# Regrouping the small matmuls of a chunked state-space scan among the matmuls of an MLP

## The chip, the cores and the metric

One NeuronCore of a Trainium2 chip runs the kernel. The metric is the device time of one execution in microseconds (us), as a median of several runs; lower is better.

## What is computed

The reference has three stages. The first is a gated linear recurrence over 4 batches, 8 heads, 768 tokens, head size 32 and state size 16, worked in chunks; the other two are an ELU MLP and a gated SiLU MLP over 3072 tokens of 256 features.

```python
# per chunk, with cum = cumsum(log a) in the chunk
CB = einsum('bhin,bhjn->bhij', C, B)
M = CB * exp(cum_i - cum_j) * causal
y = einsum('bhij,bhjd->bhid', M, x) + einsum('bhin,bhnd->bhid', C, state) * exp(cum)
state = exp(sum(la)) * state + sum_j B_j x_j * exp(cum_last - cum_j)
# then
h = y @ w_in;  g = where(h > 0, h, exp(min(h, 0)) - 1);  x = g @ w_out       # 256 -> 2048 -> 256
g = x @ w_gate; out = (silu(g) * (x @ w_val)) @ w_out                         # 256 -> 1536 -> 256
```

## The kernel before

The recurrence is cut into 24 units of 128 tokens (all 8 heads of one batch), six to a batch. Units 0 to 7 (t below CUT = 8) use halves of 64 tokens; the **later units**, 8 to 23, use the whole 128. The MLPs go over six blocks of 512 tokens. Their products are done as three fp32r products of high and low parts (a hi/lo pair: hi is a rounded copy, lo the rest).

The order of work on every engine is written out by hand. Units 0 to 3 and the first weights follow a list. Then a loop over **slots** begins: slot i runs, in this order, `m_a` (six 512-column matmuls into the PSUM tile h, of which there are two), the tasks of the list `early`, the activation of slot i and the splitting of the result of slot i-1 (ACT Relu L506, ACT copy gh L489, POOL gl L490, ACT Exp L511, DVE m L512), `m_c` of three slots before (six matmuls into c, two slots before in block 0, where it is four records of plain fp32), the list `mid`, the list `late`. Each block has 16 slots and, up to the last but one, four units of the next block: unit t has a base slot s0, the units of one block being four slots apart. An engine takes its instructions in this order and waits in place for what each needs. After the last matmuls of a block `m_end` (L535) copies c out, one half on ACT and one on DVE (L538).

The table `OFF` (L39) gives each stage of a unit its slot, counted from s0, and its list:

- `hi` (L286, ACT, late of s0-1): two copies of 128x512, B into zb and C into zc, both with one buffer. `lo` (L294, mid of s0): zb's low part on POOL, zc's on DVE.
- `scan` (L350, late of s0): decays P and E on DVE (L328, L310), then on POOL ct times P (L334) and bn times E (L348).
- `pe1` (L354, late of s0+1): the **scores**, eight matmuls of 64 rows by 128 columns into cb (L364).
- `mid` (L372, mid of s0+2): E times cb on DVE.
- `u` (L380, late of s0+2): the **state product**, eight records of 128 rows by 32 columns into columns 0 to 63 of y (L386). The last unit of a batch has none.
- `state` (L422, early of s0+3): the new state sc on DVE (L399), spread on POOL into sbd (L411) for the next unit. The last unit of a batch has none.
- `pe2` (L426, late of s0+4): the **state part**, four records of 64 rows by 128 columns (L434; none in the first unit of a batch), then the **decay products**, 16 records of 128 rows by 32 columns (L438), into columns 64 to 191 of y.
- `out` and `xl` (L457, L468, late of s0+4): y as hi/lo pair, by ACT (L466) and DVE (L470).

A matmul in plain fp32 is two records here, one in fp32r is one. Since s0+4 is the next unit's s0, a later unit's matmuls come in three separate runs between the matmuls of the MLP: scores, state product, then state part with decay products. Loads of coming units go on SP's queue and are tied to `OFF["pe1"]` (L678, L680). Two steps of decoding weights (`step_w2`) go into the slots s0+3 and one into s0+2.

Of the kernel before, what the change touches and what calls it, by code (L numbers as in the profile page):

```python
# [22 lines left out]
CUT = 8  # L23
# [13 lines left out]

BASE = -3
OFF = dict(hi=(-1, "l"), lo=(0, "m"), scan=(0, "l"), pe1=(1, "l"), mid=(2, "m"), u=(2, "l"), state=(3, "e"), pe2=(4, "l"), out=(4, "l"), xl=(4, "l"))  # L39
W2S = 16  # L40
FIRST = [0,3,6,9]
RAWB = 2
# [22 lines left out]
def ssm_mlp_glu_kernel(ctx, tc, a, bcs, xbc, w1, w2, consts, out):  # L65
# [19 lines left out]
    for f in range(NF1):  # L85
        w = W1["all", f] = [w1p.tile([128, 512], F32R, name=f"w1{s}{f}") for s in "hl"]
# [118 lines left out]
    U = {}  # L205
# [108 lines left out]
    def q0(t):  # L314

        return 0 if t % NCH > 0 else R if t < CUT else Q
# [72 lines left out]
    def a_sc(t):  # L389

        u = U[t]
        s, y, nxt = sc[t % 2], u["y"], sc[(t + 1) % 2][:, 0]
        c = t % NCH

        def step(to, of, q, w):
            if of is None:
                nc.vector.tensor_copy(to, w)
            else:
                nc.vector.scalar_tensor_tensor(to, of, u["P"][:, q - 1:q], w, ALU.mult, ALU.add)  # L399

        of = s[:, 0] if c > 0 else None
        if t < CUT:
            step(s[:, 1], of, R, y[:, 0, :2 * D])
            if c < NCH - 1:
                step(nxt, s[:, 1], Q, y[:, 1, :2 * D])
        elif c < NCH - 1:
            step(nxt, of, Q, y[:, 0, :2 * D])

    def spread(t, k, n):

        nc.gpsimd.tensor_tensor(  # L411
            sbd[t % 2][:, k:n].rearrange("p s (i q) -> p s i q", i=2),
            sc[t % 2][:, k:n].unsqueeze(2).to_broadcast([128, n - k, 2, 2 * D]),
            blk_sb.rearrange("p (i q) -> p i q", i=2).unsqueeze(1).to_broadcast([128, n - k, 2, 2 * D]), ALU.mult)

    def a_sb(t):
        if t < CUT:
            spread(t, q0(t) // R, 2)
        if t + 1 >= CUT and t % NCH < NCH - 1:
            spread(t + 1, 0, 1)  # L420

    def a_state(t):  # L422
        a_sc(t)
        a_sb(t)

    def a_y(t):  # L426


        u = U[t]
        has = t % NCH > 0  # L430
        if t >= CUT:
            for g in range(2 if has else 0):
                gs = slice(64 * g, 64 * g + 64)
                nc.tensor.matmul(u["y"][:, g, 2 * D:2 * D + Q], lhsT=sbd[t % 2][gs, 0], rhs=u["ct"][gs], start=True,  # L434
                                 stop=False)
            for h in range(H):
                g, j = divmod(h, 4)
                nc.tensor.matmul(u["y"][32 * j:32 * j + 32, g, 2 * D:2 * D + Q], lhsT=u["x"][:, 32 * h:32 * h + 32],  # L438
                                 rhs=u["E"][:, h], start=not has, stop=True)
            return  # L440
        for s in range(2):
            if s > 0 or has:
                nc.tensor.matmul(u["y"][:, s, 2 * D:2 * D + Q].rearrange("p (g q) -> p g q", g=2), lhsT=sbd[t % 2][:, s],
                                 rhs=u["ctz"][:, :, R * s:R * s + R], start=True, stop=False, skip_group_check=True)
        for g in range(2):
            y = u["y"][:, :, 2 * D + R * g:2 * D + R * g + R]
            for j in range(4):
                for s in range(2):
                    h, rs = 4 * g + j, slice(R * s, R * s + R)
                    nc.tensor.matmul(y[32 * j:32 * j + 32, s], lhsT=u["x"][rs, 32 * h:32 * h + 32], rhs=u["E"][rs, h],  # L450
                                     start=s == 0 and not has, stop=True, skip_group_check=True)

    def y_of(t):
        y = U[t]["y"][:, :, 2 * D:2 * D + Q]
        return y if t >= CUT else y.rearrange("p s (g q) -> p s g q", g=2)
# [12 lines left out]
    def a_xl(t):  # L468
        hi, lo = U[t]["hl"]
        nc.vector.tensor_tensor(lo, y_of(t), hi.bitcast(F32), ALU.subtract)  # L470
        U.pop(t)


    hps, gt, cps = {}, {}, {}
# [153 lines left out]


    STAGES = dict(hi=a_hi, lo=a_lo, scan=a_scan, pe1=a_pe1, u=a_u, state=a_state, mid=a_m, pe2=a_y, out=a_out, xl=a_xl)  # L630
    with tc.manual_schedule():
        nc.vector.memset(zero_q, 0.0)
# [9 lines left out]
        for t in range(n0 + 2):  # L642
            for nm in ("abc", "bc", "x", "ahn"):
                tok[f"L{nm}{t}"] = lambda t=t, nm=nm: a_loads(t)[nm]()
            if t < n0:
                for nm, fn in dict(cl=a_cl, mz=a_prep, E=a_E, P=a_P, ct=a_ct, bn=a_bn, cb=a_pe1, m=a_m, u=a_u, sc=a_sc,
                                   sb=a_sb, y=a_y, out=a_out, xl=a_xl).items():
                    tok[f"{nm}{t}"] = lambda t=t, fn=fn: fn(t)
# [12 lines left out]
        early, mid, pe, late = {}, {}, {}, {}  # L661
        late[8] = [(lambda: nc.scalar.activation(ident8, ident.unsqueeze(1).to_broadcast([128, H, Q]), AF.Copy), ())]

        def at(when, slot, fn, *args):
            when.setdefault(slot, []).append((fn, args))

        t = n0
        for b in range(NB - 1):
            n_u = BLOCKS[b + 1] // Q
            step = NF1 // n_u  # L670
            for k in range(n_u):
                s0 = b * NF1 + (FIRST[k] if b == 0 else k * step + BASE)
                for st, fn in STAGES.items():
                    o, w = OFF[st]
                    at(dict(e=early, m=mid, p=pe, l=late)[w], s0 + o, fn, t)
                for x in [t + 1 + (t + 1 < CUT)] if t != CUT - 2 else []:
                    if n0 + 1 < x < NU:
                        at(late, s0 + OFF["pe1"][0], a_load_x, x)  # L678
                if t + 2 < NU:
                    at(late, s0 + OFF["pe1"][0], a_load, t + 2)  # L680
                t += 1
# [20 lines left out]

        at(late, W2S - 4, load_w2)
        for i in range(W2S, last_a):
            at(late, i, step_w2, W2K[(i - BASE) % 4], NE)
# [114 lines left out]
```

## Time and profile before

| what | value |
|---|---|
| time, median of 3 runs (lowest, highest) | 668.21 us (667.93, 669.85) |
| time of the profiled execution | 666.93 us |
| its span, first to last instruction | 665.2 us |
| TensorE (PE) busy | 636.2 us, 96% |
| DVE, ACT, POOL busy | 374.6, 311.9, 312.7 us |
| granted TensorE clock, mean | 0.999 |

The span is what the trace covers; 1.73 us of the profiled execution lie around it. PE is TensorE's matmuls, PEld its weight loads, DVE the vector engine, ACT the scalar engine, POOL GpSimd, SP the engine that issues the DMAs. A line number such as L364 is that of the listing above. Busy time of PE is from the start of a matmul to its modelled end, and matmuls overlap, so a busy PE may still be slowed by changes of what it does: there the distance between starts tells more than the share.

### The profile page before, as it was taken

What the parts mean: (1) busy time and instruction counts of PE and PEld (TensorE: products, weight loads), DVE (VectorE), ACT (ScalarE), POOL (GpSimd) and SP (SyncE); (2) the same over time, 40 slices, a digit from 0 to 9 for tenths busy, and PEclk for the clock granted to TensorE, in tenths of its full rate; (3) what the DMA queues carried; (4) which work ended last, traced back from release to release, by engine and by line L of the source; (5) the groups of instructions that cost most, each with busy time, mean ns of one, the idle gap of its engine ahead of it and who ended that gap; (6) DMA issues with size and microseconds to landing.
All of it is one profiled execution on the core that took longest, in us unless ns stands there. A gap on an engine that the chain in (4) does not pass through costs nothing.

```text
span 665.2 us, 9685 instructions
## 1 busy us (share of the span) xinstructions
PE 636.2 (96%) x3620; PEld 487.6 (73%) x3620; DVE 374.6 (56%) x580; ACT 311.9 (47%) x562; POOL 312.7 (47%) x263
## 2 busy tenths in 40 slices
PE   2699999999999999999999999999999999999997
PEld 1455556776777777777778888888888888888886
DVE  5779987767677676764574663343343343343332
ACT  2155667666666666655776452332332332332322
POOL 3546656766677567774444333333333333333332
PEclk9999999999999999999999999999999999999999
DMA  5683734443443544410310000000000000000000
GB/s 177 208 290 142 214 99 126 127 148 119 132 134 107 150 129 125 152 35 17 95 49 0 1 1 0 33 0 1 32 1 0 33 1 0 33 0 1 32 1 32
DMA packets 21646, 49.54 MB, mean 74 GB/s; under 512 B 4320, under 2 KB 6496, under 8 KB 21600
## 3 DMA queue, kind: packets, MB, share of 16 engines
q1 hardware_dynamic: 21600, 48.93, 23.4%
q8 instruction: 28, 0.46, 0.3%
q14 instruction: 18, 0.15, 0.1%
HBM read 45.68 MB, written 3.24 MB: 74 GB/s over the span
## 4 chain that ended last, share of the span: by engine, by line
PE 79%; DVE 10%; ACT 4%; issue 4%; DMA 2%; SPq 1%; POOL 0%; DVEq 0%; ACTq 0%; POOLq 0%
PE h L484 16%; PE o L484 15%; PE g L484 15%; PE v L484 15%; PE c L532 14%; DMA w2e<-in_w 2%; DVE m L512 2%; DVE v L137 1%; PE cb L364 1%; DVE E L310 1%; DVE v L134 1%; PE y L438 1%; DVE v L141 1%; ACT m L511 1%; ACT m L506 1%
## 5 line engine op out<-in xcount | busy, mean ns | idle before, releaser
L490 POOL TENSOR_TENSOR gl<-m,gh 128x512 fp32r<-128x512 f32 x152 | 196.6, 1296 | 269.4 <-ACT gh L489 264.3
L604 DVE TENSOR_TENSOR m<-m,g 128x512 f32<-128x512 f32 x72 | 49.5, 688 | 169.5 <-ACT m L599 169.5
L599 ACT ACTIVATE m<-g 128x512 f32<-128x512 f32 x72 | 43.2, 599 | 191.5 <-PE g L484 191.5
L512 DVE SCALAR_TENSOR_TENSOR m<-m,h 128x512 f32<-128x512 f32 x96 | 65.4, 681 | 87.0 <-ACT m L511 85.7
L506 ACT ACTIVATE m<-h 128x512 f32<-128x512 f32 x96 | 56.9, 592 | 85.2 <-PE h L484 81.8
L489 ACT ACTIVATE gh<-m 128x512 fp32r<-128x512 f32 x152 | 94.8, 624 | 2.5 <-DVE m L512 1.3
L484 PE MATMUL h<-xh,w1h 128*128 128x512 f32 x192 | 84.0, 438 | 1.4 <-DVE xl L470 1.0
L484 PE MATMUL h<-xh,w1l 128*128 128x512 f32 x192 | 76.8, 400 | 0.0
L532 PE MATMUL c<-gh,w1h 128*128 128x512 f32 x160 | 63.5, 397 | 1.9 <-DVE x L538 1.9
L532 PE MATMUL c<-gh,w1l 128*128 128x512 f32 x160 | 63.1, 395 | 0.0
L511 ACT ACTIVATE m<-m 128x512 f32<-128x512 f32 x96 | 59.9, 624 | 0.5
L484 PE MATMUL h<-xl,w1h 128*128 128x512 f32 x192 | 60.0, 394 | 0.0
L484 PE MATMUL g<-x2h,w2h 128*128 128x512 f32 x144 | 56.8, 395 | 0.0
L484 PE MATMUL v<-x2h,w2h 128*128 128x512 f32 x144 | 56.7, 394 | 0.0
L484 PE MATMUL o<-gh,w2l 128*128 128x512 f32 x144 | 56.7, 394 | 0.0
L484 PE MATMUL o<-gl,w2h 128*128 128x512 f32 x144 | 56.7, 394 | 0.0
L484 PE MATMUL g<-x2h,w2l 128*128 128x512 f32 x144 | 56.7, 394 | 0.0
L484 PE MATMUL o<-gh,w2h 128*128 128x512 f32 x144 | 56.7, 394 | 0.0
L484 PE MATMUL v<-x2h,w2l 128*128 128x512 f32 x144 | 56.4, 392 | 0.0
L605 DVE TENSOR_TENSOR m<-m,v 128x512 f32<-128x512 f32 x72 | 49.5, 688 | 7.9 <-DVE m L604 0.5
L532 PE MATMUL c<-gl,w1h 128*128 128x512 f32 x160 | 50.3, 395 | 0.0
L484 PEld LDWEIGHTS h<-xh,w1h 128*128 128x128 f32 x192 | 36.5, 190 | 16.3 <-issue 3.2
(126 smaller groups left out, 1077.0 us busy)
## 6 DMA issues: line engine op xcount, KB each, us to landing
abc<-ac SPq DMA_DIRECT2D x16, 512.0 KB
bcraw<-in_bcs SPq DMA_DIRECT2D x32, 256.0 KB
raw<-in_w SPq DMA_DIRECT2D x15, 512.0 KB
w2e<-in_w SPq DMA_DIRECT2D x12, 512.0 KB
xb<-in_xbc SPq DMA_DIRECT2D x17, 256.0 KB
raw<-in_w SPq DMA_DIRECT2D x12, 256.0 KB
out_y<-yo SPq DMA_DIRECT2D x12, 256.0 KB
abc<-ac SPq DMA_DIRECT2D x8, 128.0 KB
```

Source lines behind the costliest of these rows:

```text
L134: nc.vector.tensor_scalar(halves(v)[:, :, 0], t["h16"][:, :, 1], 13, None, ALU.logical_shift_right)
L137: nc.vector.tensor_scalar(halves(v)[:, :, 1], t["h16"][:, :, 3], 0x8000, None, ALU.bitwise_and)
L484: nc.tensor.matmul(dst, lhsT=l, rhs=r, start=first and i == 0, stop=last and i == len(ops) - 1, **kw)
L489: nc.scalar.activation(hi, src, AF.Copy)
L490: lo_eng.tensor_tensor(lo, src, hi.bitcast(F32), ALU.subtract)
L506: nc.scalar.activation(m, h, AF.Relu, scale=-1.0)
L511: nc.scalar.activation(m, m, AF.Exp, scale=-1.0)
L512: nc.vector.scalar_tensor_tensor(m, m, -1.0, h, ALU.add, ALU.max)
L532: nc.tensor.matmul(cps[b][m], lhsT=w[:, m * 128:(m + 1) * 128], rhs=r, start=f == 0 and w is wh and r is gh, stop=f == NF1 - 1 and r is gl)
L599: nc.scalar.activation(m, pg, AF.Sigmoid)
L604: nc.vector.tensor_tensor(m, m, pg, ALU.mult)
L605: nc.vector.tensor_tensor(m, m, pv, ALU.mult)
```

## The change

Later units get a table of their own. Their hi/lo pairs are made a slot sooner (`hi` late of s0-2, `lo` mid of s0-1), the scores go from late of s0+1 to late of s0, the state product from late of s0+2 to late of s0+4 behind the decay products, and the state from early of s0+3 to early of s0+5. The list for a unit is written in the order hi, lo, scan, pe1, mid, pe2, u, out, xl, state. So late of s0+4 has, on PE: state part, decay products, state product of unit t, then the scores of unit t+1. `U.pop` is only bookkeeping of the program that writes the instructions. The loads stay tied to the old table's `pe1`. Units 4 to 7 keep the old table.

```diff
+OFF1 = dict(OFF, hi=(-2, "l"), lo=(-1, "m"), pe1=(0, "l"), u=(4, "l"), state=(5, "e"))
     def a_state(t):
         a_sc(t)
         a_sb(t)
+        if t >= CUT:
+            U.pop(t)
     def a_xl(t):
         hi, lo = U[t]["hl"]
         nc.vector.tensor_tensor(lo, y_of(t), hi.bitcast(F32), ALU.subtract)
-        U.pop(t)
+        if t < CUT:
+            U.pop(t)
-                for st, fn in STAGES.items():
-                    o, w = OFF[st]
+                off, order = (OFF, list(STAGES)) if t < CUT else (OFF1, "hi lo scan pe1 mid pe2 u out xl state".split())
+                for st in order:
+                    fn, (o, w) = STAGES[st], off[st]
                     at(dict(e=early, m=mid, p=pe, l=late)[w], s0 + o, fn, t)
```

## Rows read from the trace of the kernel before

**Rows 1.** The page: busy time of PE, and the chain by engine.
```profile
PE 636.2 (96%) x3620; PEld 487.6 (73%) x3620; DVE 374.6 (56%) x580; ACT 311.9 (47%) x562; POOL 312.7 (47%) x263
...
PE 79%; DVE 10%; ACT 4%; issue 4%; DMA 2%; SPq 1%; POOL 0%; DVEq 0%; ACTq 0%; POOLq 0%
```

**Rows 2.** Timeline of PE, 239 to 253 us (start, us, instructions): scores, state product.
```profile
240.87 0.66 PE L364 MATMUL cb<-zc,zb 64*128 64x128 f32 x8
241.47 0.50 PE L484 MATMUL h<-xh,w1h 128*128 128x512 f32 x1
...
244.45 0.32 PE L386 MATMUL y<-xb 128*32 128x64 f32 x8
244.70 0.50 PE L484 MATMUL h<-xh,w1h 128*128 128x512 f32 x1
```

**Rows 3.** The same timeline, a slot without small matmuls: c to h, h to h.
```profile
247.13 0.63 PE L532 MATMUL c<-gl,w1h 128*128 128x512 f32 x2
247.59 0.39 PE L484 MATMUL h<-xh,w1h 128*128 128x512 f32 x1
247.82 0.40 PE L484 MATMUL h<-xh,w1l 128*128 128x512 f32 x1
```

**Rows 4.** The same timeline, the run of state part and decay products.
```profile
249.91 0.63 PE L532 MATMUL c<-gl,w1h 128*128 128x512 f32 x2
250.47 0.49 PE L434 MATMUL y<-xb,sbd 64*128 64x128 f32 x4
250.89 0.64 PE L438 MATMUL y<-E,xb 128*32 128x128 f32 x16
251.46 0.50 PE L484 MATMUL h<-xh,w1h 128*128 128x512 f32 x1
251.80 0.40 PE L484 MATMUL h<-xh,w1l 128*128 128x512 f32 x1
```

**Rows 5.** Tile y: shortest, median and longest ns of one record, first and last start.
```profile
L438 PE MATMUL y<-E,xb x256: 272/273/297, 102.6 to 305.8; 128*32 128x128 f32 x128
...
L386 PE MATMUL y<-xb x120: 219/243/313, 11.5 to 286.0; 128*32 128x64 f32 x104, 64*32 64x64 f32 x16
...
L434 PE MATMUL y<-xb,sbd x56: 272/322/374, 102.1 to 305.3; 64*128 64x128 f32 x56
```

**Rows 6.** Timeline of all engines, 236 to 253 us: DVE.
```profile
238.95 0.70 DVE L298 TENSOR_TENSOR zc<-bcraw,zc 128x512 fp32r<-128x512 f32 x1
...
241.01 2.26 DVE L310 TENSOR_TENSOR_SCAN E<-abc,ident 128x1024 f32<-128x1024 f32 x1
...
243.19 0.65 DVE L512 SCALAR_TENSOR_TENSOR m<-m,h 128x512 f32<-128x512 f32 x1
...
247.54 0.27 DVE L399 SCALAR_TENSOR_TENSOR sc<-sc,P,y 128x64 f32<-128x64 f32 x1
```

**Rows 7.** The waits: engine line <- waited for, us in total, times, longest.
```profile
PE c L532 <- DVE x L538: 1.9, 3, 0.9
```

**Rows 8.** Timeline of DVE, 74 to 112 us, at the first later unit.
```profile
87.56 0.68 DVE L512 SCALAR_TENSOR_TENSOR m<-m,h 128x512 f32<-128x512 f32 x1
...
90.09 1.36 DVE L298 TENSOR_TENSOR zc<-bcraw,zc 128x512 fp32r<-128x512 f32 x1
```

**Rows 9.** Timeline of PE, 87 to 96 us, at the first later unit.
```profile
87.70 0.45 PE L450 MATMUL y<-E,x 64*32 64x64 f32 x32
...
91.60 0.66 PE L364 MATMUL cb<-zc,zb 64*128 64x128 f32 x8
```

**Rows 10.** Timeline of all engines, 236 to 253 us: ACT and POOL.
```profile
247.89 0.46 POOL L411 TENSOR_TENSOR sbd<-sc,con 128x128 f32<-128x128 f32 x1 [1.49 <-DVE sc L399]
247.99 0.71 ACT L292 ACTIVATE zb<-bcraw,con 128x512 fp32r<-128x512 f32 x1
...
248.31 1.29 POOL L490 TENSOR_TENSOR gl<-m,gh 128x512 fp32r<-128x512 f32 x1
...
251.95 1.75 POOL L298 TENSOR_TENSOR zb<-bcraw,zb 128x512 fp32r<-128x512 f32 x1
```

## The prediction

> **What bounds the kernel now.** I read the page first: PE is busy for 96% of the span and carries 79% of the chain that ended last; no other engine has more than 10% of that chain [rows 1]. So time is won or lost where PE is held up or switched, in the stretch in which the later units run, from about 90 to 306 us. The timeline of PE there is what the forecast rests on, and the reader should look at distances between starts, not at busy time. In a slot without small matmuls the last two c matmuls begin .46 us before the first h, and h follows h after .23 [rows 3]. Around a run of small matmuls both distances grow: c pair to first small matmul .56 (250.47 - 249.91), first h to second h .34 (251.80 - 251.46) [rows 4]. **The edges of a run cost .10 + .11 = .21 us**, whatever is in it. On top comes a drain after its last matmul, since the next shape starts only later. It is worked out from the start of a group, plus its busy time, minus the duration of one record (a median where the run is long, the shortest where the group's records differ): the last decay product starts at 250.89 + .64 - .27 = 251.26, the h behind it at 251.46, so .20; the last state product at 244.45 + .32 - .22 = 244.55, h at 244.70, so .15; the last state part at 250.47 + .49 - .27 = 250.69, the decay products of another shape at 250.89, again .20 [rows 2, 4, 5]. A unit pays these edges three times.
>
> **The change, part by part.** *State product behind the decay products.* Both are 128 rows by 32 columns, so no change of shape lies between them. The 16 decay records start within 251.26 - 250.89 = .37 us, in four groups of four, so .12 from group to group; I let the state product follow as a fifth group. Gained per unit: the edges .21 and the drain .20 less that step of .12, together **.29 us**. The eight records themselves are as many as before.
>
> *Scores of the next unit behind that.* Gained: the edges .21 and the state product's own drain .15, but now the scores come after a change of shape. The trace has no such step. Its nearest row is state part to decay products, small to small, at .20, and I take it; the ends are .12, as if no shape changed, and .33, which is what the first small matmul costs behind a 512-column one (.56 less the .23 between the two c). Net .21 + .15 - .20 = **.16 us** (.03 to .24). Where a batch's last unit has no state product, the scores follow the decay products: .21 + .20 - .20 = .21.
>
> *Counting.* I leave out the three units at block 0's end for now. State products join in units 9, 10, 12 to 16 and 18 to 22: 12 x .29 = 3.5 us. Scores of units 10 to 23 join, 12 behind a state product and 2 behind decay products: 12 x .16 + 2 x .21 = 2.3 us. Together **5.8 us**.
>
> *Pairs a slot sooner.* The two ACT copies of .71 each [rows 10], zb's low part on POOL and zc's on DVE are as many as before. What they leave is the slot in which DVE has most to do: behind zc (.70) it runs xl, P, E (2.26) and only then m of the next slot, at 243.19 to 243.84, which frees an h buffer that PE takes at 244.70 [rows 2, 6]. Without zc this chain is .70 earlier, with the state step that now comes in front of that m (.27) later: .43 earlier in all. PE arrives earlier too, by about half a microsecond, since the edges and drains between are gone; a margin of .86 stays about .8, so this costs nothing. If that cover went, h would wait in 14 units.
>
> *Block ends.* In the slot after such an E, DVE also copies half of c, and PE waits for it: three times, 1.9 us in all [rows 7]. With DVE .43 earlier and PE's arrival there about as now (the scores that stood in that slot now stand just ahead of it), each wait loses .4: **1.2 us** gained (0 to 1.9).
>
> *Moved waits and queues.* The state is made two slots later; sbd is wanted by the next unit's state part, three slots on, so nothing waits. POOL makes sbd (.46 [rows 10]) after bn instead of two slots later, ahead of a gl that is used two slots on, and its queue there is .7 earlier for zc's sake. SP's queue: the loads are not moved, but the load of x into the buffer that the state product still reads waits for it, some .3 us longer; behind it in the queue stand loads that wait for the end of E anyway. I cost both at nothing. Hi copies read a raw load one slot sooner than now; it is issued five slots ahead of that, and no ACT wait for it shows among the longest waits, so nothing again.
>
> *Block 0's end.* Here I expect a loss. The scores of unit 8 would naturally follow the decay products of unit 7 (87.70 to 88.15) but need zc, and DVE, filled with decoding weights, is free for it only after m at 87.56 + .68 = 88.24; zc takes 1.36 there, so to 89.6 [rows 8, 9]. PE waits some 1.3 us in its run. Three joins give .21 + .29 + .16 = .66 back. That would be a loss of .6, or of nothing if the following slots take it up (now too the scores wait there: they start at 91.60, zc ends at 91.45); **I take .3** (.64 lost to .66 gained).
>
> **The sum.** 5.8 + 1.2 - .3 = **6.7 us**. From the profiled execution, 666.93, that makes 660.2. The median of the three runs shown is 668.21, 1.28 more than the profiled one, and I forecast in its terms: 668.21 - 6.7 = **661.5 us**.
>
> **A rule against it.** The starts of a group show that the small matmuls overlap and that .21 us of a run lie outside of them [rows 3, 4]. The Trainium skill, page "TensorEngine Tiling (Array Packing)", section Performance Considerations (Instruction Overhead), says that each matmul has about 60 cycles of overhead. By that rule the price goes with the number of matmuls, which this change keeps, and the sum would be 0 for the joins. The trace does not bear it out as the whole price: the distances .56 against .46 and .34 against .23 belong to the edges. It stands as the first rival.
>
> **The rivals.**
>
> *Price by the matmul.* If edges and drains come back inside the long run (every change of shape as dear as .33, or the weight loads of the longer run not hidden), only the block ends are left: 668.2 - 1.2 = 667.0, within .3% of now. For it: the run still has two changes of shape inside it. Against: state part to decay products costs .20, less than an edge and a drain together. Chance .11.
>
> *The pair becomes the last wait (slower).* The scores now stand inside a run, and a late zb holds the whole of it, with the MLP's next slot behind. Place: POOL's queue. Had zb been put behind the gl that runs at 248.31 to 249.60, it would end at 249.60 + 1.75 = 251.35; the scores come at about 251.26 + .12 + .10 + .20 = 251.68 [rows 4, 10]. That is a margin of .33, and .75 with sbd (.46) gone from ahead of that gl. It decides from there: a wait of .48 us in each of 14 units eats the 6.7, of .62 makes it measurably slower. If one more gl (1.29) comes ahead of zb, the wait is about .7 to .9 and the time 668.2 - 6.7 + 14 x .7 to .9 = 671 to 674. For it: gl and zb stand in a row on POOL, 3 us together, in a slot that is itself under 3 us long. Against: zb has the state part, the decay products and the state product ahead of it as cover. Chance .08.
>
> *Half the gain.* Scores at the dear end (.03 instead of .16), block ends unchanged, block 0 losing in full: 6.7 - 1.6 - 1.2 - .3 = 3.6 gained, so 664.6. Chance .14. The cheap ends together (scores at .12, block ends 1.9, block 0 +.66) give 6.7 + 1.2 + .7 + 1.0 = 9.6, so 658.6; that belongs to the forecast.
>
> **How the numbers follow.** The forecast has .67, half the gain .14, no change .11, slower .08. The bounds of the forecast and of half the gain give 658.6 to 664.6; with half a microsecond for the spread of the median (the runs lie 1.9 apart) the range is 658.0 to 665.0, and leaves out the first two rivals. About .3%, 2.0 us, is what a measurement of this kernel can tell from none, so faster means below 666.2: forecast and half the gain, .81; same is the first rival, .11; slower the second, .08.
>
> **What would show it.** In the profile after, PE's timeline of a later unit should have three plain slots and one with L434, L438, L386 and L364 in one run; from the state part's start to the next h should be about .42 + .37 + .12 + .10 + .20 + .60 = 1.8 us (the last is the scores' own, 240.87 to 241.47 [rows 2]), the starts of h and c elsewhere as now. L386 should begin about .12 after the last decay product, L364 about .20 after the last L386. The waits of c for x on DVE should be near .7 in sum. Wrong would be: a gap ahead of L364 put down to POOL zb or DVE zc in every unit; L386 starting only after a drain; h waiting for m; or the small matmuls of the run further apart than now.

## The result and the profile after

The changed kernel takes **661.78 us** (median of 4 runs, 660.43 to 662.88), the kernel before 668.07 in the same comparison: ratio .9905, 95% interval .9889 to .9922. So it is 6.3 us faster; 661.5 was forecast, 6.7 less than before. The profiled execution of the changed kernel took 662.88 us (span 661.1). Of the ten runs of it that there are in all, six show a mean granted clock of .999 or 1.000 and a median of 661.3 us, four one of .996 or .997, both profiled ones among them, and 662.5.

The page first: its busy time and chain, as in [rows 1].

```profile
PE 628.7 (95%) x3620; PEld 491.6 (74%) x3620; DVE 386.7 (58%) x580; ACT 312.0 (47%) x562; POOL 315.3 (48%) x263
...
PE 79%; DVE 9%; DMA 4%; issue 2%; ACT 2%; POOL 2%; SPq 1%; DVEq 0%; POOLq 0%; ACTq 0%
```

PE still bounds the kernel; as many matmuls take 7.5 us less busy time. Where that comes from is seen in the timeline of PE over one run of a later unit (start, us, instructions), which answers to [rows 2] and [rows 4]; the last line is the h behind the next unit's run.

```profile
248.62 0.63 PE L537 MATMUL c<-gl,w1h 128*128 128x512 f32 x2
249.18 0.49 PE L438 MATMUL y<-xb,sbd 64*128 64x128 f32 x4
249.60 0.65 PE L442 MATMUL y<-E,xb 128*32 128x128 f32 x16
250.06 0.29 PE L388 MATMUL y<-xb 128*32 128x64 f32 x8
250.28 0.66 PE L366 MATMUL cb<-zc,zb 64*128 64x128 f32 x8
250.88 0.50 PE L489 MATMUL h<-xh,w1h 128*128 128x512 f32 x1
251.22 0.39 PE L489 MATMUL h<-xh,w1l 128*128 128x512 f32 x1
...
263.90 0.50 PE L489 MATMUL h<-xh,w1h 128*128 128x512 f32 x1
```

All four kinds stand in one run. From its start to h are 250.88 - 249.18 = 1.70 us (1.8 forecast). The last decay product starts at 249.60 + .65 - .27 = 249.98, the state product .08 later (.12 forecast). The last state product starts at 250.06 + .29 - .22 = 250.13, the scores .15 later (.20 forecast). A unit's period is 263.90 - 250.88 = **13.02 us**; in the kernel before it is 13.58, from the h at 251.46 [rows 4] to the h behind the next unit's same products:

```profile
265.04 0.50 PE L484 MATMUL h<-xh,w1h 128*128 128x512 f32 x1
```

DVE and POOL around that run, in the timeline of all engines, as in [rows 6] and [rows 10]:

```profile
247.51 0.80 DVE L300 TENSOR_TENSOR zc<-bcraw,zc 128x512 fp32r<-128x512 f32 x1
...
247.72 1.74 POOL L300 TENSOR_TENSOR zb<-bcraw,zb 128x512 fp32r<-128x512 f32 x1
...
252.10 2.26 DVE L312 TENSOR_TENSOR_SCAN E<-abc,ident 128x1024 f32<-128x1024 f32 x1
...
254.29 0.25 DVE L401 SCALAR_TENSOR_TENSOR sc<-sc,P,y 128x64 f32<-128x64 f32 x1
254.46 0.67 DVE L517 SCALAR_TENSOR_TENSOR m<-m,h 128x512 f32<-128x512 f32 x1
```

zb ends at 249.46, .82 us ahead of the scores (.33 to .75 forecast). m ends at 255.13; the h that needs its buffer comes two slots behind the one at 250.88, at 256.55, 1.42 us later (about .8 forecast), so nothing waits. The waits of c for its copy on DVE have halved, 1.9 [rows 7] to .9:

```profile
PE c L537 <- DVE x L543: 0.9, 3, 0.5
```

### The profile page after: what moved, and what is told of

Its sections match the earlier page's. It is cut to its first block, busy times and chain, and to the rows that moved or that the text cites. A ratio compares the mean times of both kernels' runs of the same rounds, so it can differ in the third digit from the quotient of the medians.

```text
span 661.1 us, 9674 instructions
## 1 busy us (share of the span) xinstructions
PE 628.7 (95%) x3620; PEld 491.6 (74%) x3620; DVE 386.7 (58%) x580; ACT 312.0 (47%) x562; POOL 315.3 (48%) x263
## 4 chain that ended last, share of the span: by engine, by line
PE 79%; DVE 9%; DMA 4%; issue 2%; ACT 2%; POOL 2%; SPq 1%; DVEq 0%; POOLq 0%; ACTq 0%
PE o L489 15%; PE g L489 15%; PE v L489 15%; PE h L489 15%; PE c L537 14%; DMA w2e<-in_w 2%; DMA raw<-in_w 2%; DVE E L312 2%; DVE m L517 1%; DVE v L139 1%; PE y L442 1%; PE c L531 1%; PE cb L366 1%; DVE v L136 1%; DVE v L143 1%
## 5 line engine op out<-in xcount | busy, mean ns | idle before, releaser
L495 POOL TENSOR_TENSOR gl<-m,gh 128x512 fp32r<-128x512 f32 x152 | 199.4, 1314 | 261.4 <-ACT gh L494 259.7
L489 PE MATMUL h<-xh,w1h 128*128 128x512 f32 x192 | 81.7, 426 | 1.3 <-DVE xl L474 1.0
```

Source lines behind the costliest of these rows:

```text
L489: nc.tensor.matmul(dst, lhsT=l, rhs=r, start=first and i == 0, stop=last and i == len(ops) - 1, **kw)
L495: lo_eng.tensor_tensor(lo, src, hi.bitcast(F32), ALU.subtract)
```

## The experiments

**The changed kernel and the kernel before, each once more.** No edit. What was expected of the changed kernel:

> The changed kernel once more, unchanged, for a second trace of it. Theory (edges and drains of the runs are saved): the steady slots repeat to .05 us, 4.57 + 2.89 + 2.78 + 2.78 us per unit against 13.57 before, and whatever differs from the first trace lies ahead of the first later unit (before about 90 us) or in the late stages. Ratio to before .989 to .992. Rival (the change itself delays the start, so that its first 90 us are slower in every execution): h of the slot in which unit 7's last products run again starts 5 us later than in the kernel before.

and of the kernel before:

> The kernel before once more, for a second trace of it. Theory: steady slots as in the first trace (3.58, 3.23, 2.89, 3.87 us); how much later or earlier the first later unit begins than in the first trace (scores of unit 8 at 91.6 us) tells how far the start of the kernel varies without any change. Rival (the start is fixed for a kernel): the scores of unit 8 are again at 91.6 us within .3.

The changed kernel took 661.80 us (661.09 to 663.37), ratio .9899 (.9876 to .9922); the kernel before, in a single run, 668.52. From the slot with unit 9's last products to the h behind the last unit's run, the first pair of traces has 194.39 and 186.85 us, the second 194.37 and 186.84: **7.5 us, to .02**. (Unit 9's state product lies ahead of this stretch before and inside it after, so moving the later units gains some .45 us more than that.) The start is what varies. In the kernel before the scores of unit 8 start at 91.60 [rows 9] in one trace and at 93.94 in the other; the slot that ends with unit 7's last products starts at 83.66 and 85.98 there, at 88.81 and 85.46 in the changed kernel. A start that is 5 us later in every execution of the changed kernel, the rival, is out; so is a fixed start. But 7.5 us gained and only 6.3 measured leave more than a microsecond lost ahead of that stretch. The first later unit, unit 8, lies there, and the second trace of the changed kernel bears on it. ACT, POOL and PE there:

```profile
85.41 0.71 ACT L294 ACTIVATE zb<-bcraw,con 128x512 fp32r<-128x512 f32 x1
86.03 0.72 ACT L294 ACTIVATE zc<-bcraw,con 128x512 fp32r<-128x512 f32 x1
86.64 0.62 ACT L175 ACTIVATE w1h<-v 128x512 fp32r<-128x512 f32 x1
```
```profile
87.34 1.83 POOL L179 TENSOR_TENSOR w1l<-v,w1h 128x512 fp32r<-128x512 f32 x1 [3.58 <-ACT w1h L175]
89.12 1.59 POOL L413 TENSOR_TENSOR sbd<-sc,con 128x256 f32<-128x256 f32 x2
90.68 1.26 POOL L300 TENSOR_TENSOR zb<-bcraw,zb 128x512 fp32r<-128x512 f32 x1
```
```profile
90.36 0.71 PE L447 MATMUL y<-x,sbd 128*128 128x128 f32 x4 [1.22 <-POOL sbd L413]
...
92.00 0.68 PE L366 MATMUL cb<-zc,zb 64*128 64x128 f32 x8 [0.55 <-POOL zb L300]
```

The copies for unit 8's pair stand ahead of a weight's copy on ACT; behind that copy POOL's low part of the weight waits, behind it the spreading of unit 7's state, and for that unit 7's state part on PE. PE waits 1.22 us and then .55 for zb. The same stretch by microseconds (us, PE busy and matmuls, granted clock, DMA share, GB/s):

```profile
89.00:90.00 1.00, 0.14 (x1) 1.00 0.26 100
90.00:91.00 1.00, 0.64 (x4) 1.00 0.21 84
91.00:92.00 1.00, 0.46 (x33) 1.00 0.03 12
92.00:93.00 1.00, 1.00 (x9) 0.76 0.00 0
93.00:94.00 1.00, 1.00 (x3) 0.50 0.00 0
```

Behind these two waits, from 92 us on, the granted clock falls from 1.00 (2.4 GHz) to .50 (1.2 GHz). In neither trace of the kernel before does it fall here.

The first trace of the changed kernel loses most of its time elsewhere. There the clock falls sooner, behind a wait ahead of unit 7's state product:

```profile
84.32 0.47 PE L388 MATMUL y<-x 64*32 64x64 f32 x16 [2.29 <-issue]
```
```profile
85.00:86.00 1.00, 1.00 (x3) 0.50 0.76 262
```

That is not the sooner pair's doing: the kernel whose pairs are not sooner (the last run below) has such a wait, 2.76 us, and such a fall at the same place. PE then comes late to unit 7's run, does not wait for sbd, and waits only the .55 us for zb. From the start of slot 13, which holds unit 7's run, to that of unit 9's slot the first trace takes 27.06 us, the second 30.01, the kernel before 28.0. So the chain through ACT and POOL ends in a wait of PE in one trace of two, and what unit 8 costs on average is for more runs to say. Two runs below test it.

**Only the state product moved.**

```diff
-OFF1 = dict(OFF, hi=(-2, "l"), lo=(-1, "m"), pe1=(0, "l"), u=(4, "l"), state=(5, "e"))
+OFF1 = dict(OFF, u=(4, "l"), state=(5, "e"))
```

> Only the state product and the state are moved (state product behind the decay products, state two slots later); scores and pairs stay where they were. Theory: 12 to 13 joins of .32 us each are saved (.21 edges, .20 drain, .09 for the step in its place), 3.9 to 4.2 us; the three waits of c for its copy on DVE become some .2 to .3 us longer each, as the state step now comes ahead of that copy and nothing is taken off DVE. Together 3.2 to 3.8 us faster than before, about 664.6. In the trace the slot with the state product shrinks from 3.23 to 2.78 us and the slot with state part and decay products grows from 3.87 to about 3.99. Rival (price by the matmul): no change, 668, the 3.87 us slot growing by the .45 that the other loses.

Measured 665.00 us, ratio .9944 (.9924 to .9963): 3.5 us faster, as the theory said. The slot that held the state product is 2.89 us, 2.78 and the .11 of the h behind a run, the slot with the run 3.98. Its rows on PE:

```profile
170.00 0.64 PE L442 MATMUL y<-E,xb 128*32 128x128 f32 x16
170.46 0.29 PE L388 MATMUL y<-xb 128*32 128x64 f32 x8
170.69 0.50 PE L489 MATMUL h<-xh,w1h 128*128 128x512 f32 x1
```

The decay products end up followed after .09 by the state product (170.00 + .64 - .27 = 170.37 to 170.46), and h comes at 170.69 where without it, .20 behind the last decay product, it would be 170.57: eight matmuls for .12 us instead of .45. The waits of c grow only from 1.9 to 2.1.

**Only the scores and their pairs moved.** The list of a unit has its state product and state ahead of `mid` again; `U.pop` is as in the kernel before.

```diff
-OFF1 = dict(OFF, hi=(-2, "l"), lo=(-1, "m"), pe1=(0, "l"), u=(4, "l"), state=(5, "e"))
+OFF1 = dict(OFF, hi=(-2, "l"), lo=(-1, "m"), pe1=(0, "l"))
...
-"hi lo scan pe1 mid pe2 u out xl state".split()
+"hi lo scan pe1 u state mid pe2 out xl".split()
```

> Only the scores and their pairs are moved (scores behind the decay products of the unit before, pairs a slot sooner); state product and state stay. Theory: 14 to 15 joins of .21 us (edges .21; the drain .20 is replaced by a change of shape of about .20), 3.0 us; the three waits of c for its DVE copy, 1.9 us in all before, shrink by up to .7 each as zc's low part leaves that slot, so 1.0 to 1.9 less. Together 4 to 5 us faster than before, about 663.6. In the trace the slot with the scores shrinks from 3.58 to 2.89 and the 3.87 slot grows to about 4.4 to 4.5. Rival (the pair becomes the last wait): the scores start more than .25 us after the last decay product in most units, waiting for POOL zb, and the time is 667 or more.

Measured 666.79 us, ratio .9974 (.9957 to .9990): 1.7 us faster where 4 to 5 were expected. The slots are as the theory had them, 2.89 and 4.46, and the waits of c fall to 1.3; of the scores only those of unit 8 and, by .2 us, of unit 10 wait for zb. From unit 9's slot to the h behind the last run the trace is 3.3 us shorter than the first of the kernel before, so the joins pay, and the rest of the miss lies at unit 8 again: PE waits 1.21 us for sbd and .54 for zb, and the mean granted clock is .85 from 85 to 95 us and .81 from 95 to 105. (This is the trace of the slowest of the twelve runs, 669.21 us; the median lost less.) The state product's move does not take part in that loss: with it alone slots 13 and 14 take 4.61 and 3.90 us, as in the kernel before. The sooner pair does.

**Unit 8 on the old table.**

```diff
-                off, order = (OFF, list(STAGES)) if t < CUT else (OFF1, ...
+                off, order = (OFF, list(STAGES)) if t <= CUT else (OFF1, ...
```

(and the two conditions on `U.pop` likewise).

> As the changed kernel, but unit 8 keeps the old table: its pairs, scores, state product and state stay where they were before, and the new order begins with unit 9. Theory (the pairs of unit 8 a slot sooner come among the last weights of block 0: the two ACT copies hold up the copy of a weight, POOL's low part of that weight and the spreading of unit 7's state come later, and PE waits 1 to 2 us in unit 7's run, once long enough to lose clock): slots 13 to 18 are as in the kernel before, 25.1 us from the start of slot 13 to that of slot 19, less .2 for one join; no half clock between 85 and 105 us; steady slots as in the changed kernel. So 1 to 2.5 us faster than the changed kernel, about 660, ratio to before .985 to .988. Rival (the start of the kernel varies by itself and unit 8 costs nothing): 661.8 to 662.5, as the changed kernel or slower by the two joins that are lost.

Measured **659.56 us** (659.28 to 660.30), ratio .9862 (.9836 to .9889), 2.2 less than the changed kernel, whose ten runs all lie above (660.43 to 663.37). The granted clock is 1.00 from 85 to 105 us, and slots 13 to 16 take 4.62, 3.91, 3.53 and 2.81 us, against 4.63, 3.90, 3.54 and 2.81 in the first trace of the kernel before. So moving unit 8 costs 2.2 us net of the two joins that it brings. The clock is the smaller part of it: against the six runs of the changed kernel with a clock of .999 or 1.000 it is still 1.7.

**Unit 8's copies behind the weight's.** The changed kernel, with the two ACT copies one place later in the same slot's list:

```diff
+                    if st == "hi" and t == CUT:
+                        continue
                     at(dict(e=early, m=mid, p=pe, l=late)[w], s0 + o, fn, t)
...
+        at(late, 11, a_hi, CUT)
         last_a = (NB - 1) * NF1 - 1
```

> As the changed kernel, but on ACT the two copies for unit 8's pair stand behind the copy of the weight of that slot instead of ahead of it; nothing else is moved. Theory (they hold up that weight's copy, POOL's low part of it, and behind that the spreading of unit 7's state): that low part starts some 1.3 us sooner, unit 7's state part no longer waits for POOL sbd, and the clock stays at full speed between 85 and 105 us; 1 to 2 us faster than the changed kernel, 660 to 661. Rival (unit 8's loss is the wait of its scores for zb or zc alone): slots 13 and 14 stay as slow as in the changed kernel, 661.8.

Measured 660.57 us (660.24 to 660.97), ratio .9876 (.9860 to .9892): 1.2 less than the changed kernel. The ranges overlap, so the time alone would not settle it; the trace shows what is gone. ACT, POOL and PE at the same place:

```profile
85.14 0.61 ACT L175 ACTIVATE w1h<-v 128x512 fp32r<-128x512 f32 x1
```
```profile
85.83 1.29 POOL L179 TENSOR_TENSOR w1l<-v,w1h 128x512 fp32r<-128x512 f32 x1 [2.36 <-ACT w1h L175]
87.09 1.51 POOL L413 TENSOR_TENSOR sbd<-sc,con 128x256 f32<-128x256 f32 x2
```
```profile
88.68 0.61 PE L447 MATMUL y<-x,sbd 128*128 128x128 f32 x4
...
90.98 0.66 PE L366 MATMUL cb<-zc,zb 64*128 64x128 f32 x8 [1.31 <-DVE zc L300]
```

The state part no longer waits and the clock stays up. What is left is the wait of the scores for zc, 1.31 us, the wait that the prediction had priced at 1.3. So unit 8 loses in two ways: this wait or the one for zb, and, in the second trace of the changed kernel and that with only the scores moved, one of 1.2 us that comes through ACT and POOL, after which the clock fell.

**The state product first in the run.** On top of unit 8 on the old table; three changes of shape inside the run instead of two.

```diff
-"hi lo scan pe1 mid pe2 u out xl state".split()
+"hi lo scan pe1 mid u pe2 out xl state".split()
```

> As the run with unit 8 on the old table, but the state product comes ahead of the state part, so that the run has three changes of shape inside it instead of two and the same matmuls. Theory (a change of shape costs a drain): state product to state part .15, decay products to scores .20 instead of .09 for the step from decay products to state product and .15 to the scores; .13 to .15 us more per unit, 12 units, 1.6 to 1.8 us slower than that run; the slot with the run grows from 4.57 to 4.70. Rival (price by the matmul, or one price per run whatever is in it): the slot stays 4.57.

Measured 661.81 us (660.11 to 662.30), ratio .9889; the run's slot is 4.71 instead of 4.57, in each of the units with all four kinds.

```profile
168.55 0.32 PE L388 MATMUL y<-xb 128*32 128x64 f32 x8
168.80 0.49 PE L438 MATMUL y<-xb,sbd 64*128 64x128 f32 x4
169.22 0.64 PE L442 MATMUL y<-E,xb 128*32 128x128 f32 x16
169.80 0.66 PE L366 MATMUL cb<-zc,zb 64*128 64x128 f32 x8
170.39 0.50 PE L489 MATMUL h<-xh,w1h 128*128 128x512 f32 x1
```

The same matmuls in another order cost .14 us more in such a run: the state part, the decay products and the scores each now stand behind a change of shape. (The medians are 2.2 us apart; the traces, from unit 9's slot on, 1.1, since the block ends give a little back.) A price by the matmul cannot do that. The first rival falls here. The rule of some 60 cycles for each matmul (the Trainium skill, page "TensorEngine Tiling (Array Packing)", Performance Considerations, Instruction Overhead) may hold for each, but in this trace it is not the whole price: order alone moves that by .14 us.

**The scores in the middle of the run.** On top of unit 8 on the old table, with `a_y` called in two parts so that the next unit's scores come behind the state part, of the same shape (the conditions in `a_y` that make the two parts are left out here):

```diff
+                    if st == "pe2" and t > CUT:
+                        at(late, s0 + o, fn, t, (0,))
+                        at(late, s0 + o, fn, t, (1,))
+                        continue
+                    if st == "pe1" and t > CUT + 1:
+                        k0 = next(j for j, (f, z) in enumerate(late[s0 + o]) if f is a_y and z[1:] == ((1,),))
+                        late[s0 + o].insert(k0, (fn, (t,)))
+                        continue
```

> As the run with unit 8 on the old table, but the next unit's scores come right behind the state part, both of 64 rows by 128 columns, and ahead of the decay products: one change of shape inside the run instead of two. Theory: state part to scores about .11 (a step, no drain), scores to decay products .20, state product to h .15; about .09 us less per unit than that run, slot 4.48, 1.0 to 1.3 us faster in all, if the pair is ready; zb ends .5 to .9 us before the scores now and the scores come .65 us sooner, so in units without that much some .1 us of waiting comes back. Rival A (fp32 behind fp32r drains like a change of shape): no gain, 4.57. Rival B (the pair or m is late: out comes .4 us later, and m with it, against a margin of .8 for the h buffer): slots of 4.7 or more, or h waiting for m in every unit, 1 us slower or more.

Measured 659.41 us (658.36 to 661.36), ratio .9865 (.9838 to .9892): not to be told from the run without it. Where the pair is ready the slot is 4.38, .19 less and twice what was expected; elsewhere the scores wait for zb, and slots of 4.99 and 4.38 us (where the unit has no state part and 4.15 was there before) give it back. Both kinds of run, the first with a wait:

```profile
116.86 0.66 PE L366 MATMUL cb<-zc,zb 64*128 64x128 f32 x8 [0.35 <-POOL zb L300]
...
168.55 0.49 PE L438 MATMUL y<-xb,sbd 64*128 64x128 f32 x4
168.80 0.64 PE L366 MATMUL cb<-zc,zb 64*128 64x128 f32 x8
```

**The same with the pairs yet a slot sooner.**

```diff
-OFF1 = dict(OFF, hi=(-2, "l"), lo=(-1, "m"), pe1=(0, "l"), u=(4, "l"), state=(5, "e"))
+OFF1 = dict(OFF, hi=(-3, "l"), lo=(-2, "m"), pe1=(0, "l"), u=(4, "l"), state=(5, "e"))
```

> As the run with the scores right behind the state part, with the pairs of units 9 to 23 one slot sooner still (two slots sooner than in the kernel before). Theory (there the state part and the scores overlap, .025 us from start to start where the pair was ready, and the rest was waiting for zb): every run's slot 4.38, none with a wait for zb; against the run with unit 8 on the old table .19 us less in each of 14 units, 2.0 to 2.7 us faster than it, 657.0 to 657.6, ratio to before .982 to .985. Rival (ACT's copies and POOL's low part hit a slot that is full already, the one with E times scores, or m is late for the h buffer since out comes later): h waits for m or c for gl, 659.5 or more.

Measured **657.44 us** (657.03 to 659.72), ratio .9829 (.9813 to .9845): the fastest of all, 4.3 us under the changed kernel and 11 under the kernel before. The slot is 4.37 to 4.38 in the units with all four kinds and 4.15 to 4.16 where there is no state part; none waits for zb. From unit 9's slot on its trace is 2.0 us shorter than that with unit 8 on the old table.

```profile
169.21 0.49 PE L438 MATMUL y<-xb,sbd 64*128 64x128 f32 x4
169.45 0.65 PE L366 MATMUL cb<-zc,zb 64*128 64x128 f32 x8
170.03 0.65 PE L442 MATMUL y<-E,xb 128*32 128x128 f32 x16
170.49 0.29 PE L388 MATMUL y<-xb 128*32 128x64 f32 x8
170.71 0.50 PE L489 MATMUL h<-xh,w1h 128*128 128x512 f32 x1
```

**The pairs not sooner.** The changed kernel, with the pairs in their old slot:

```diff
-OFF1 = dict(OFF, hi=(-2, "l"), lo=(-1, "m"), pe1=(0, "l"), u=(4, "l"), state=(5, "e"))
+OFF1 = dict(OFF, pe1=(0, "l"), u=(4, "l"), state=(5, "e"))
```

> As the changed kernel, but the pairs stay in their old slot (ACT copies late of the slot before s0, low parts in s0), so the low part zb is made in the very slot whose run holds the scores. Theory (the pair a slot sooner is what lets the scores stand in the run): zb needs h of that slot, Relu, gh, gl and then 1.3 to 1.75 us on POOL; the scores wait 1.7 to 2.8 us in each of 15 units, 25 to 40 us, 687 to 702 in all, unless it loses clock as well; put down to POOL zb. Rival (the order alone matters, the pair is hidden anyway): 661 to 664.

Measured 717.32 us, ratio 1.0729 (1.0699 to 1.0759), more than expected. One run of it, and the clock behind it by microseconds (columns as above):

```profile
189.60 0.29 PE L388 MATMUL y<-xb 128*32 128x64 f32 x8
191.98 0.66 PE L366 MATMUL cb<-zc,zb 64*128 64x128 f32 x8 [2.08 <-POOL zb L300]
```
```profile
192.00:193.00 1.00, 1.00 (x10) 1.00 0.10 35
193.00:194.00 1.00, 1.00 (x6) 0.83 0.00 0
194.00:195.00 1.00, 1.00 (x4) 0.50 0.00 0
195.00:196.00 1.00, 1.00 (x4) 0.50 0.55 131
```

PE waits for zb in 14 runs, 31.9 us in all, and for zc at units 8 and 9, 3.4 us, which is within what was expected; the clock is most of the rest. After all but two of these runs it falls to .50 in the slot behind, which then takes 4.2 to 4.5 us instead of 2.89; that is some 18 us in twelve slots. The pair a slot sooner is no side matter of the change: without it the change would be slower by far than the slow rival of the prediction, 671 to 674 us, which had waits of .7 to .9 us and nothing of the clock.

## Why the prediction was right, and where it was not

**Edges and drains (5.8 us).** Right in kind, a little small. The state product follows the decay products after .08 to .09, not .12, and the scores follow the state product after .15, not .20. So a join of a state product gives .21 + .20 - .09 = .32 instead of .29, and one of scores .21 + .15 - .15 = .21 instead of .16: 12 x .32 + 14 x .21 = 6.8 us. The state product's move alone gains 3.5 us; the trace of the scores' move alone gains 3.3 from unit 9's slot on, while its time gains 1.7; and the order with a third change of shape shows that a change of shape inside a run is paid for.

**Block ends (1.2 us).** The waits of c on DVE lost 1.0.

**Covers.** zb, m, sbd and the loads stayed hidden in every steady slot, with margins no smaller than those worked out: zb .82 against .33 to .75, m 1.42 against about .8.

**Block 0's end (.3 us lost, at most .64).** This is the step that failed. The prediction had the wait of unit 8's scores for zc, and the run with the copies behind the weight's shows it at 1.31. What it did not follow was ACT: it costed the two copies at nothing, since they are as many as before and their load is there in time. But at unit 8 they stand ahead of a weight's copy, and behind that copy POOL's queue holds the sbd for unit 7's state part; PE waited 1.22 us for it in the second trace, and the clock fell. Neither is in the prediction. Leaving unit 8 out gains 2.2 us; with the joins that unit 8 brings (.21 + .32) the move costs some 2.7 where the prediction had the 1.3 of the wait.

That the sum came so near is in part luck. Joins of 6.8 and block ends of 1.0 leave, of the measured 6.3, a loss of 1.5 at the start instead of .3: joins 1.0 too small and a loss 1.2 too small cancel. Two of its side figures do not follow from their rows: behind one more gl the margins of .33 and .75 give a wait of .54 to .96 us, not .7 to .9, and scores at the cheap end give 14 x .08 = 1.1, not 1.2. The forecast does not hang on either.

**The rivals.** Price by the matmul is refuted by order alone. The pair as the last wait is real at unit 8, and in every run of units 9 to 23 once the pair is left in its old slot. Half the gain had the scores at .03; they gave .21.

## What to carry to other kernels

Here the small matmuls between large ones are paid by the run and by the change of shape, so put them into one run and sort them by shape; that is worth .56 us a unit in this order and .75 with the scores beside the state part. Whatever lets them stand together has to be ready at the earliest of them, and a wait inside such a run costs PE the wait and then, in twelve of the 14 runs of the kernel with late pairs, the clock. When a steady pattern is shifted by a slot, follow its first unit through every engine's queue: the neighbours there are other ones than in the pattern.

## What was not expected of the hardware

State part and scores, fp32 and fp32r, have the same shape of 64 rows by 128 columns, and between them there is no step of .12 as between groups of the decay products: the last state part starts at 168.55 + .49 - .27 = 168.77, the scores at 168.80. So the change of data type has no drain here.

The clock fell after a wait of 2.08 us in front of the scores in the kernel with late pairs, and at unit 8 after waits of 1.22 and .55 us with 36 small matmuls, 1.1 us, between them. Another wait of 2.08 us in the kernel with late pairs, ahead of the scores at 126.09, left it at 1.00, and so did the wait of 1.31 us in the run with unit 8's copies behind the weight's. So the length of one wait does not settle it. The many steady runs of small matmuls, 1.70 us long, left it at 1.00.

The first 84 us of one and the same kernel differ by 2.3 us between the two traces of the kernel before and by 3.4 between those of the changed one; in the four traces ACT waits there 1.83 to 3.62 us for a weight's DMA.
